# Two small matmul visits made into one, and two opening batches put in another order, in a fused attention and expert kernel

## The chip, the cores and the metric

One core of one Trainium2 chip. The metric is the device time of one execution in microseconds (us), median over several executions, the kernel before run on the same chip in the same rounds. The granted clock is the share of TensorE's full clock that the profile shows as granted, as a mean over an execution or a stretch. Times inside an execution are those of the profile, counted from the start of the span.

## The reference

```python
# q, k, v: (8 batches, 8 heads, 576 positions, 64)
scores = (q @ k.T) / 8
mask_local   = (rel >= 0) & (rel < 32)             # heads 0 to 3
mask_strided = (rel >= 0) & (pos_k % 32 == pos_q % 32)   # heads 4 to 7
attn = softmax(where(mask, scores, -1e9)) @ v
x = attn as (4608 tokens, 512)
h = x @ w_in                                       # 512 -> 2048
g = maximum(h, 0) + alpha * minimum(h, 0)
out = g @ w_out                                    # 2048 -> 512, float32
```

The sum of a softmax comes as a 65th column of v that is all ones, so after PV one reciprocal and one multiply on VectorE (DVE) divide.

## The kernel before

The expert part runs in nine chunks of 512 tokens: first layer in 16 groups (`hps`), second in 16 pieces (`ops`). Between them "pieces" of attention for later batches are slipped in: transposes (T), scores (S, two per head pair), PV (P, two or three per pair), transposes of the result (X). The kernel keeps the instructions of each engine in the order written. Pairs are numbered through the batches, four to a batch, so pairs 8 to 11 are batch 2. From batch 2 on, the results of three pairs of a batch are transposed by a transfer (`x_dma`) and that of the fourth by PE (X): of batch 2, `xs` holds pair 10, and X is done for pair 11. PSUM is split in three pools: `ps` (3 banks: PV, transposes), `hps` (3 banks) and `sp` (2 banks).

```python
def score_piece(P, i):                # a pair is two heads; i is the half of the positions
    sp = pbpool.tile([128, 2, 512], F32, tag="sp")
    ...
    for x, t in enumerate(grp):
        for y in range(2):            # two heads on the two 64-row halves of the array
            nc.tensor.matmul(sps[y][...], P.kT[64*y:64*y+64, ...], P.qT[64*y:64*y+64, ...])
    nc.scalar.activation(ev, sp, AF.Exp, scale=SCALE)         # ACT
    nc.gpsimd.tensor_tensor(ev, ev, m, op=ALU.mult)           # POOL: the mask

def pv_piece(P, a):
    pv = pspool.tile(...); ...        # matmuls
    nc.vector.reciprocal(rc, pv[..., 64])
    nc.vector.tensor_tensor(P.x16[...], pv[..., 0:64], rc, op=ALU.mult)

def lin1_piece(n, m):
    hps = phpool.tile(...); ...       # 4 matmuls
    nc.scalar.activation(neg, hps, AF.Relu, scale=-1.0)
    def fin(): nc.vector.scalar_tensor_tensor(gTs[n][:, m, :], neg, oma, hps, ...)  # frees hps
    late.append(fin)

def attn_step(end):
    if pos["i"] < end:
        pieces[pos["i"]][1]()         # one attention piece
        pos["i"] += 1
    while late:
        late.pop(0)()                 # then fin of the first-layer group

def x_dma(P):   ... nc.sync.dma_start_transpose(P.xs, P.x16[0:80, :])     # a strided pair
def x_copy(P):  ... nc.scalar.copy(xT[...], P.xs[...])                     # on ACT, later
```

The softmax here doesn't subtract the row's maximum and nothing guards it: scores larger than these inputs give would overflow.

## Time and profile before

| | us |
|---|---|
| time, median of 3 before the change was tried | 329.38 |
| span of the profiled execution, whose time was 328.5 | 326.6 |
| TensorE (PE) busy | 316.8 |
| first expert matmul starts | 26.56 |
| first layer of chunks 3 and 4 starts | 135.76 and 169.12 |

The distance between two chunks is the length of a steady cycle, 33.36 us, in which one batch of attention is slipped in.

### The profile page before, as it was taken

To read this page: it belongs to the slowest core of one execution; us is meant where nothing else is said; L and a number is where in the kernel's file an instruction comes from. 1 tells how busy PE (TensorE), PEld (TensorE's weight loads), DVE (VectorE), ACT (ScalarE), POOL (GpSimd) and SP (SyncE) were. 2 spreads that over 40 slices of the span, in tenths; PEclk is the share of its full clock that TensorE was granted. 3 is DMA by queue.
4 is the path that set the end of the run, shared out by engine and by line. 5 is a ranking of instruction groups with operands and counts; after the bars stand their busy time and mean duration, and the time that the engine had idled before them with its cause. 6 is when DMAs were issued, how large, how long until landed. Compare 5 with 4: busy or idle time off the path is not lost.

```text
span 326.6 us, 6269 instructions
## 1 busy us (share of the span) xinstructions
PE 316.8 (97%) x2493; PEld 161.8 (50%) x2493; DVE 182.8 (56%) x358; ACT 172.5 (53%) x295; POOL 141.2 (43%) x152
## 2 busy tenths in 40 slices
PE   7899999999998999999999999999999999999995
PEld 2454455554553445444568744445444444444444
DVE  5477835577543872488338832883377338505801
ACT  2744663368446754575467545764566347415610
POOL 8832495307996366736573638342513300000000
PEclk9999999999999999999999999999999999999999
DMA  6999999797499899686967496635530320021011
GB/s 222 198 206 207 243 210 170 115 258 167 90 155 155 214 81 153 118 212 74 160 109 222 59 143 116 109 43 101 122 76 0 55 91 25 1 91 40 0 64 64
DMA packets 77596, 40.32 MB, mean 123 GB/s; under 512 B 58480, under 2 KB 69248, under 8 KB 77568
## 3 DMA queue, kind: packets, MB, share of 16 engines
q0 software_dynamic: 41728, 17.38, 51.7%
q1 hardware_dynamic: 35840, 22.55, 28.5%
q8 instruction: 19, 0.31, 0.4%
q14 instruction: 9, 0.07, 0.1%
HBM read 38.01 MB, written 9.44 MB: 145 GB/s over the span
## 4 chain that ended last, share of the span: by engine, by line
PE 92%; DVE 3%; ACT 2%; DMA 2%; issue 0%; SPq 0%; DVEq 0%; ACTq 0%
PE hps L544 39%; PE ops L585 37%; PE sp L295 4%; PE pv L345 4%; PE tp L235 2%; DMA ql<-in_q_dram 2%; PE wps L607 1%; PE ops L577 1%; PE xp L362 1%; DVE x L354 1%; PE sph L311 1%; PE sp L311 1%; ACT kT L175 1%; DVE qT L177 1%; PE sph L295 1%; ACT qT L175 0%
## 5 line engine op out<-in xcount | busy, mean ns | idle before, releaser
L585 PE MATMUL ops<-wout,gT 128*128 128x512 f16 x560 | 137.7, 379 | 0.0
L557 DVE SCALAR_TENSOR_TENSOR gT<-neg,oma,hps 128x512 f16<-128x512 f32 x144 | 106.0, 745 | 54.6 <-ACT neg L554 47.1
L544 PE MATMUL hps<-xT,win 128*128 128x512 f16 (+1 forms) x640 | 133.4, 358 | 1.4 <-ACT xT L366 1.2
L554 ACT ACTIVATE neg<-hps 128x512 f32<-128x512 f32 x144 | 86.0, 597 | 41.0 <-PE hps L544 39.5
L329 POOL TENSOR_TENSOR et<-et,consts 128x576 f16<-128x576 f16 (+1 forms) x48 | 61.1, 1274 | 91.8 <-ACT et L319 91.8
L544 PEld LDWEIGHTS <-win 128*128 128x128 f16 x640 | 59.6, 98 | 57.6 <-issue 2.7
L585 PEld LDWEIGHTS <-gT 128*128 128x128 f16 x560 | 48.4, 97 | 45.6
L319 ACT ACTIVATE et<-sp 72x576 f16<-72x576 f32 (+1 forms) x56 | 36.2, 646 | 45.0 <-PE sp L295 36.7
L352 DVE RECIPROCAL rc<-pv 72x6 f32<-72x6 f32 (+2 forms) x80 | 14.8, 185 | 51.2 <-PE pv L345 51.2
L590 ACT COPY osb<-ops 128x512 f32<-128x512 f32 x35 | 20.5, 585 | 31.6 <-PE ops L585 31.2
L354 DVE TENSOR_TENSOR x<-pv,rc 96x384 f16<-96x384 f32 (+2 forms) x62 | 33.0, 532 | 2.1
L345 PEld LDWEIGHTS <-et 72*128 72x128 f16 (+1 forms) x448 | 23.2, 98 | 16.2 <-DVE x L354 1.1
L295 PEld LDWEIGHTS <-kT 64*128 64x128 f16 x448 | 10.8, 95 | 25.8 <-issue 20.7
L295 PE MATMUL sp<-qT,kT 64*128 64x72 f16 (+1 forms) x392 | 17.0, 201 | 1.9 <-ACT kT L175 1.9
L607 PE MATMUL wps<-wrm 128*128 128x512 f16 x44 | 16.1, 440 | 1.2 <-DVE wrm L619 1.2
L167 POOL DMA_DIRECT2D vl<-in_v_dram x8 | 11.2, 1397 | 9.9 <-PE pv L345 8.6
L345 PE MATMUL pv<-vs,et 72*128 72x65 f16 x256 | 15.3, 194 | 0.1
L177 DVE COPY qT<-tp 128x1024 f16<-128x1024 f16 (+1 forms) x10 | 10.1, 1011 | 7.9 <-PE tp L235 7.9
L179 POOL COPY vs<-stv 72x1024 f16<-72x1024 f16 x14 | 14.4, 1034 | 0.0
L383 ACT COPY xT<-xs 128x576 f16<-128x576 f16 x6 | 7.8, 1300 | 7.7 <-DMA xs<-x16s 7.7
L345 PE MATMUL pv<-vl,et 128*128 128x65 f16 x192 | 10.8, 194 | 0.0
L175 ACT COPY kT<-tp 128x1024 f16<-128x1024 f16 (+1 forms) x10 | 8.4, 843 | 3.9 <-PE tp L235 3.9
(72 smaller groups left out, 162.6 us busy)
## 6 DMA issues: line engine op xcount, KB each, us to landing
out_dram<-osb SPq DMA_DIRECT2D x35, 256.0 KB, 2.2
ql<-in_q_dram SPq DMA_DIRECT2D x6, 512.0 KB, 4.9
kl<-in_k_dram SPq DMA_DIRECT2D x6, 512.0 KB, 5.1
stv<-in_v_dram POOLq DMA_DIRECT2D x8, 288.0 KB, 6.4
vl<-in_v_dram POOLq DMA_DIRECT2D x6, 384.0 KB, 10.4
win<-in_moe_w_in_dram POOLq DMA_DIRECT2D x4, 512.0 KB, 9.3
wout<-in_moe_w_out_dram POOLq DMA_DIRECT2D x4, 512.0 KB, 16.6
qsd<-in_q_dram POOLq DMA_DIRECT2D x6, 288.0 KB, 5.7
```

What stands on the lines that cost most here:

```text
L295: keep(nc.tensor.matmul(sps[y][:, w * x : w * x + w], P.kT[hf, k0 : k0 + 128], P.qT[hf, q0 : q0 + w], start=(x == 0), stop=(x == len(grp) ...
L319: keep(nc.scalar.activation(ev.rearrange("r (y c) -> r y c", y=2), sp[0:r, :, 0:n], AF.Exp, scale=SCALE))
L329: keep(nc.gpsimd.tensor_tensor(ev, ev, m, op=ALU.mult))
L345: keep(nc.tensor.matmul(pv[:, 65 * x : 65 * x + 65], et[0:r, c : c + 128], v16[0:r, 2 * P.pr + hh, t, :] if P.strided else v16[:, 6 * (2 * ...
L352: keep(nc.vector.reciprocal(rc[0:w, 0:nb], pvv[:, :, 64]))
L354: keep(nc.vector.tensor_tensor(P.x16[0:w, c0 : c0 + 64 * nb].rearrange("r (c e) -> r c e", e=64), pvv[:, :, 0:64], rc[0:w, 0:nb].unsqueeze ...
L544: keep(nc.tensor.matmul(hps[:, dst : dst + w], win16[:, kk, 128 * m : 128 * m + 128], xT[:, kk, src : src + w], start=(kk == 0 and x == 0) ...
L554: keep(nc.scalar.activation(neg, hps, AF.Relu, scale=-1.0))
L557: keep(nc.vector.scalar_tensor_tensor(gTs[n][:, m, :], neg, oma[:, m : m + 1], hps, op0=ALU.mult, op1=ALU.add))
L585: keep(nc.tensor.matmul(ops, gTs[n][:, kf, 128 * mt : 128 * mt + 128], wout16[:, kf, :], start=(kf == 0), stop=(kf == 15)))
L590: keep(nc.scalar.copy(osb, ops))
L607: keep(nc.tensor.matmul(wps, wrm[:, 0:128], wrm, start=True, stop=True))
```

## The change

Its intent: each score piece puts TensorE into row-tiled mode and back, so do both pieces of a pair in one visit (batches 2 to 7), with the second half in banks of `ps` and its exponentials deferred, one by one, to the ends of this step and the next. In batches 0 and 1, start PV of the strided pairs between the transposes of the local ones, and let ACT do one of the local copies.

```diff
+    def score_both(P):
+        for i in range(2):
+            if i:
+                sps = [pspool.tile([128, 512], F32, tag="ps", name="sph") for _ in range(2)]
+            else:
+                sp = pbpool.tile([128, 2, 512], F32, tag="sp", name="sp")
...
+            if i == 0:
+                keep(nc.scalar.activation(..., sp[0:r, :, 0:n], AF.Exp, scale=SCALE))
+                keep(nc.gpsimd.tensor_tensor(mv, mv, m, op=ALU.mult))
+                continue
+            defer.extend([lambda: ex(0), lambda: ex(1)])     # halves on ACT, mask after the second
...
-            seq.append(("S", Sc(a, 0)))
+            seq.append(("S", lambda a=a: score_both(pairs[a])))
...
-        if okA:
-            seq.append(("S2", Sc(a, 1)))
...
-        copyP = next((i for i, z in enumerate(seq) if z[0] == "S2"), 0)
+        copyP = min(2, len(seq) - 1)
...
         while late:
             late.pop(0)()
+        if defer:
+            defer.pop(0)()
...
+        fns += [Pv(A[0], 0), T(u1, "q"), Pv(A[0], 1), T(u1, "k"), Pv(A[0], 2), Sc(L[0], 0), Sc(L[0], 1)]
+        fns += [lambda: (over_v(...), pv_piece(pairs[A[1]], 0)), Sc(L[1], 0), Pv(A[1], 1)]
...
```

More of the change, by code (lines that the diff above doesn't have):

```diff
@@ L329, in score_piece, with ex @@
         keep(nc.gpsimd.tensor_tensor(ev, ev, m, op=ALU.mult))
+    defer, defer_et = [], {}
+    def score_both(P):
+        w, r = P.w, 72 if P.strided else 128
+        for i in range(2):
+            et = ets[ectr["i"] % NE]
+            ectr["i"] += 1
+            if i:
+                sps = [pspool.tile([128, 512], F32, tag="ps", name="sph") for _ in range(2)]
+            else:
+                sp = pbpool.tile([128, 2, 512], F32, tag="sp", name="sp")
+                sps = [sp[:, y] for y in range(2)]
+            grp = P.sgroups[i]
+            n = w * len(grp)
+            for x, t in enumerate(grp):
+                if P.dx:
+                    q0 = k0 = 80 * (4 * (2 * P.pr + t % 2) + t // 2)
+                else:
+                    q0, k0 = w * t, 32 + 72 * t if P.strided else 96 * t
+                for y in range(2):
+                    hf = slice(64 * y, 64 * y + 64)
+                    keep(nc.tensor.matmul(
+                        sps[y][:, w * x : w * x + w], P.kT[hf, k0 : k0 + 128],
+                        P.qT[hf, q0 : q0 + w], start=(x == 0), stop=(x == len(grp) - 1),
+                        skip_group_check=True))
+                    P.et[(2 * (t // 2) + y, t % 2) if P.strided else (t, y)] = (et, n * y + w * x)
+            ev = et[0:r, 0 : 2 * n]
+            if not P.strided and i == 0:
+                mv = ev.rearrange("r (y c) -> r y c", y=2)
+                m = mfirst.unsqueeze(1).to_broadcast([r, 2, n])
+            else:
+                mv = ev.rearrange("r (c f) -> r c f", f=w)
+                m = (mstr if P.strided else mother).unsqueeze(1).to_broadcast([r, 2 * n // w, w])
+            if i == 0:
+                keep(nc.scalar.activation(
+                    ev.rearrange("r (y c) -> r y c", y=2), sp[0:r, :, 0:n], AF.Exp, scale=SCALE))
+                keep(nc.gpsimd.tensor_tensor(mv, mv, m, op=ALU.mult))
+                continue
+            def ex(y):
+                keep(nc.scalar.activation(
+                    ev[:, n * y : n * y + n], sps[y][0:r, 0:n], AF.Exp, scale=SCALE))
+                if y:
+                    keep(nc.gpsimd.tensor_tensor(mv, mv, m, op=ALU.mult))
+            defer_et["et"] = et
+            defer.extend([lambda: ex(0), lambda: ex(1)])
@@ L331, in pv_piece @@
     def pv_piece(P, a):
+        while defer and any(P.et[z][0] is defer_et["et"] for z in P.et):
+            defer.pop(0)()
         if P.x16 is None:
@@ L369, in x_piece @@
         else:
-            keep(nc.vector.tensor_copy(xT[:, P.hp, base : base + S], xp[:, 0:576]))
+            cast_copy("act" if P.b < NEARLY and P.hp == 0 else "dve",
+                      xT[:, P.hp, base : base + S], xp[:, 0:576])
     def x_dma(P):
@@ L404, in X, with alone @@
         return lambda: x_piece(pairs[g])
-    def alone(u0, u1, ahead):
+    def alone(u0, u1):
         A, L = (2 * u0, 2 * u0 + 1), (2 * u1, 2 * u1 + 1)
-        feed(T(u0, "q"), -1)
-        feed(T(u0, "k"), -1)
-        for g in A:
-            for i in range(2):
-                feed(Sc(g, i), -1)
-        if ahead:
-            feed(T(u1, "q"), -1)
-            feed(T(u1, "k"), -1)
-            for i in range(2):
-                feed(Sc(L[0], i), -1)
-        for g in A:
-            for i in range(3):
-                feed(Pv(g, i), -1)
-        if not ahead:
-            feed(T(u1, "q"), -1)
-            feed(X(A[0]), -1)
-            feed(T(u1, "k"), -1)
-            feed(X(A[1]), -1)
-            for i in range(2):
-                feed(Sc(L[0], i), -1)
-        for i in range(2):
-            feed(Sc(L[1], i), -1)
-        if ahead:
-            for g in A:
-                feed(X(g), -1)
-        for g in L:
-            for i in range(2):
-                if g == L[0] and i == 0:
-                    feed(lambda: (over_v(u0 // 2, "dve"), pv_piece(pairs[L[0]], 0)), -1)
-                else:
-                    feed(Pv(g, i), -1)
-        for g in L:
-            feed(X(g), -1)
-    alone(1, 0, True)
+        fns = [T(u0, "q"), T(u0, "k")] + [Sc(g, i) for g in A for i in range(2)]
+        fns += [Pv(A[0], 0), T(u1, "q"), Pv(A[0], 1), T(u1, "k"), Pv(A[0], 2), Sc(L[0], 0), Sc(L[0], 1)]
+        fns += [lambda: (over_v(u0 // 2, "dve"), pv_piece(pairs[A[1]], 0)), Sc(L[1], 0), Pv(A[1], 1)]
+        fns += [Sc(L[1], 1), Pv(A[1], 2), Pv(L[0], 0), X(A[0]), Pv(L[0], 1), X(A[1])]
+        fns += [Pv(L[1], 0), Pv(L[1], 1), X(L[0]), X(L[1])]
+        for fn in fns:
+            feed(fn, -1)
+    alone(1, 0)
     end0 = len(pieces)
-    alone(3, 2, True)
+    alone(3, 2)
     end1 = len(pieces)
@@ L529, in attn_step @@
             late.pop(0)()
+        if defer:
+            defer.pop(0)()
     gTs = {}
```

## The prediction

> **What bounds the kernel now.** I read the page first (busy time, the row of forty slices, the chain that ended last), then the sums by stretches of 20 us, then the chain in order of time, and last the timeline wherever the chain leaves TensorE.
>
> ```profile
> PE 316.8 (97%) x2493; PEld 161.8 (50%) x2493; DVE 182.8 (56%) x358; ACT 172.5 (53%) x295; POOL 141.2 (43%) x152
> ...
> PE 92%; DVE 3%; ACT 2%; DMA 2%; issue 0%; SPq 0%; DVEq 0%; ACTq 0%
> ```
>
> TensorE (PE) is 92% of the chain that ended last; no other engine is near full on average. So a change pays only if it shortens PE's own work, or removes one of the few waits of PE. Where are those? From the stretches (first value span, then PE busy):
>
> ```profile
> 0.00:20.00 20.00, 16.83 (x156) 8.38 (x157) 10.85 (x34) 9.03 (x18) 15.55 (x29) 1.00 1.22 209
> 20.00:40.00 20.00, 19.34 (x145) 9.52 (x145) 15.81 (x31) 10.81 (x20) 6.07 (x9) 1.00 1.25 214
> 40.00:60.00 20.00, 19.16 (x209) 10.62 (x208) 9.49 (x23) 10.40 (x24) 13.83 (x17) 1.00 1.76 194
> 60.00:80.00 20.00, 19.81 (x155) 10.10 (x154) 14.00 (x25) 12.39 (x23) 7.20 (x8) 1.00 1.05 196
> 80.00:100.00 20.00, 20.00 (x202) 10.42 (x201) 11.52 (x28) 8.13 (x14) 19.21 (x19) 1.00 1.15 118
> 100.00:120.00 20.00, 18.81 (x139) 8.68 (x137) 13.62 (x25) 15.03 (x25) 11.56 (x11) 1.00 0.70 149
> 120.00:140.00 20.00, 20.00 (x167) 9.86 (x165) 8.29 (x18) 10.50 (x17) 11.25 (x12) 1.00 1.40 133
> ```
>
> From 120 to 240 us PE has no idle time. Idle are 3.17 us at the start, 0.66 and 0.84 us in batches 0 and 1, 0.19 us in 60:80, 1.19 us just after 100 us. In 80:100 GpSimd (POOL, fifth engine) is 96% full, which matters below. Within the gapless part, the chain shows what a visit to attention costs the stream of expert matmuls:
>
> ```profile
> 111.39 1.73 PE hps L544 x8
> 113.12 0.24 PE sp L295 x8
> 113.36 1.83 PE hps L544 x8
> 115.19 0.18 PE pv L345 x6
> 115.38 1.73 PE hps L544 x8
> ```
>
> Eight expert matmuls of 512 columns take 1.73 us after a PV visit (L345), but 1.83 after a score visit (L295): a score visit costs about 0.10 us in the group beside it besides its own 0.24. A PV visit adds nothing beyond its 0.18 us.
>
> **What the Trainium skill says.** "TensorEngine Tiling (Array Packing)", section Key Properties: changing the tiling mode drains TensorE. Scores use 64-row halves (contraction over head_dim 64), all else uses the full array; the trace agrees, as single starts read from it show. The last expert matmul before a score visit starts at 154.506 us and the first score at 154.818: 0.312 us where the stream otherwise goes at 0.216, so 0.096 us lost going in. The last score pair starts at 154.923 and the next expert matmul at 155.054, 0.131 us later where the pairs are 0.033 apart, then 0.227 instead of 0.216 to the next: about 0.11 us coming out. "TensorE: Matmul & The Clock Gate", section The mechanism (Part 3), says matmuls of different row groups start about 4 ns apart; here the two halves of a head pair start 3 to 4 ns apart. Same page, section "Architectural detail: the array is 16× 32×32, not 1× 128×128", says ACT and DVE are strict FIFO; the trace shows a copy held behind another at 100 us (below). "PSUM — Partial Sum Buffer", section Specifications, gives 8 banks per partition; the kernel's pools hold all (3+3+2), which is why the second half of a merged visit must borrow banks of the pool that PV and transposes use.
>
> **The change, part by part.**
>
> Part 1, one visit per pair. From batch 2 on there are 6 x 4 = 24 head pairs, each with two score visits before and one after. A strided visit costs 0.24 + 0.10 = 0.34 us; of this its four concurrent pairs stream 4 x 0.034 = 0.135, so 0.205 us is entry and exit. A local visit: 0.23 + 0.10 = 0.33, three pairs about 0.045 apart, 0.135, so 0.195. Merged, the second half pays streaming only. All of it lies on PE, which is the path: 24 x 0.20 = **4.9 us** off.
>
> What it adds: the second half's exponential becomes two of 288 columns instead of one of 576. From batches 0 and 1: 0.41 us each with 0.29 between starts, so 0.70 for the two against 0.65 for one; 24 x 0.05 to 0.15 is under 4 us on ACT, which has 45% idle. It doesn't delay the evictions of the first layer: taking PE free after a first-layer group as zero, ACT's relu of that group occupies 0.2 to 0.7, the wide exponential 0.7 to 1.25, the first half 1.25 to 1.55, and the next group (0.475 us visit plus 0.863) is ready at 1.54. The other half is deferred behind the next relu, 2.03 to 2.33, and the next group is ready at 2.40. So no loss, provided the deferral works as written. Banks: the visit takes two of three in the shared pool. I followed the rotation through one batch; each taker comes at least one 0.86 us step after the half that frees its bank, so no regular wait.
>
> Part 2, batches 0 and 1. The end of batch 0 was a chain of DVE work, one multiply after another 0.69 us apart with a reciprocal between:
>
> ```profile
> 24.90 0.55 DVE x L354
> ...
> 25.59 0.57 DVE x L354
> ...
> 26.54 0.47 DVE xT L370
> ...
> 27.05 13.76 PE hps L544 x63
> ```
>
> Before, DVE starts its ten PV pieces at 17.93. The new order lets the first at 13.9, between the local transposes. I laid the new order out by hand with these durations (PV 0.20, warm-up matmul 0.22, score visit with mask about 0.69, transposed copies 0.69 DVE and 0.58 ACT): the local transposes' copies now queue behind PV's DVE work, local scores start about 16.7 instead of 16.04, four score visits and six PVs then alternate until about 21, and the last multiply ends near 24.75 instead of 26.16. The first expert matmul comes at about 25.65: **1.4 us** off. One local copy moved to ACT leaves DVE's tail. In batch 1 PE waits 0.37 and 0.47 us for the transposed copies; with PV pieces between, I expect **0.6 us** of the 0.84 back. The loads batch 1 needs landed by 39.2 us (issue 23 plus 15.8 and so on), used no sooner than 40.6, so they don't eat the gain.
>
> Part 3, pacing. A batch has 17 pieces in place of 21. At the start of batch 2 scores come two first-layer groups after the key transpose instead of one, which takes back the 0.2 to 0.3 us PE wait in 60:80: **0.25 us**.
>
> Part 4, given back in batch 2. The 1.19 us just after 100 us:
>
> ```profile
> 100.14 1.30 ACT L383 COPY xT<-xs 128x576 f16<-128x576 f16 x1 [3.73 <-DMA xs<-x16s]
> ...
> 101.35 0.58 ACT L590 COPY osb<-ops 128x512 f32<-128x512 f32 x1
> ...
> 101.83 0.65 ACT L319 ACTIVATE et<-sp 128x576 f16<-128x576 f32 x1
> ...
> 102.37 0.64 ACT L366 COPY xT<-xp 128x576 f16<-128x576 f16 x1
> ```
>
> ACT was held by a transposing transfer (6.3 us to landing), and everything queued behind it reached PE. After the change that transfer is issued about one second-layer step (1.15 us) earlier relative to the batch's end, but two more exponentials (0.6 us) stand before the last copy, and PE's own transpose now needs the bank that the first of them frees. By hand the stall becomes 1.75 us: **0.5 us** lost. And in 75:90, where POOL is nearly full, the second mask of a pair now queues behind casts (1.03 us each); PV of the first two pairs of batch 2 may wait 0.3 to 0.5 us for it twice, of which I count **0.5 us**.
>
> Sum: 4.9 + 1.4 + 0.6 + 0.25 - 0.5 - 0.5 = 6.15 us. 329.4 - 6.15 = **323.2 us**, 1.9% faster.
>
> **Rivals.**
> (a) Banks or ACT become the new wait: if a PV or transpose waits for the deferred half in each pair, 24 x 0.2 eats part 1, and the time is about 327 to 328. For it: two of three shared banks, and ACT's chain at 100 us. Against: ACT is 53% busy, and steps are 0.86 us apart.
> (b) Batch 0's gain is hidden because the start is bound by loads (DMA share 1.2 there): then about 324.6. For: the software queue is busy until 40 us. Against: the chain at 17 to 27 us is DVE and PE, with no transfer in it.
> (c) The batch 2 stall shrinks rather than grows, as the transfer lands sooner, and POOL keeps up: then 321.5 to 322.
>
> **Range and chances.** Part 1 is arithmetic on PE's path, good to 0.5 us. Parts 2 and 3 together 1.2 to 3.0; part 4 between +0.8 and -2.5. This gives 321.0 to 326.0 for eight in ten. 2% faster is 322.8, just beside my middle, with the losses more likely under- than overestimated: faster 0.42, within 2% 0.57, slower 0.01.
>
> **What would show it.** L295's successor should show 16 or 12 matmuls in one visit of about 0.37 us in the chain plus 0.10 beside it, 24 of them; a steady batch cycle should fall from 33.4 us (102.8 to 135.9 on to 169.3) by 0.8 us to about 32.6. The first expert matmul should start near 25.6 instead of 27.05, and the waits of PE for key copies in 40:60 mostly vanish. PE idle near the end of batch 2 should be 1.2 to 2.3 us, released by ACT. I am wrong if the steady cycle falls by less than 0.5 us (rival a), if the first expert matmul still starts at 27 (rival b), or if the batch 2 stall is gone (rival c).

## The result, and the profile after

| | before | changed |
|---|---|---|
| median of 6 executions each | 329.22 us | 328.01 us |
| ratio of means, 95% interval | | 0.9966 (0.9952 to 0.9979) |
| granted clock | 1.0 (profiled execution) | 0.993 to 0.995 (all six) |

A ratio here and below is the mean time of one kernel's runs over that of the other's runs of the same rounds, so not quite the ratio of the medians quoted. The change brings 0.3%, not 1.9%: 328.01 us lies above the range of 321.0 to 326.0, and the prediction is wrong.

Busy time and the chain by engine, changed kernel:

```profile
PE 314.9 (96%) x2493; PEld 162.9 (50%) x2493; DVE 182.4 (56%) x356; ACT 173.1 (53%) x321; POOL 140.8 (43%) x152
...
PE 85%; issue 4%; DMA 4%; DVE 2%; POOL 2%; ACT 1%; SPq 0%; POOLq 0%; ACTq 0%; DVEq 0%
```

The chain by engine has lost 7 points of PE and gained DMA and "issue" (time with no wait that the profile can name). The loss has a place. The same stretches as before, at the end of batch 2 (after the span the busy times of PE, PEld, DVE, ACT and POOL, then the granted clock, DMA share and GB/s):

```profile
80.00:100.00 20.00, 17.81 (x190) 9.45 (x191) 9.45 (x24) 6.95 (x15) 18.81 (x19) 1.00 0.98 118
100.00:120.00 20.00, 17.93 (x124) 8.14 (x124) 11.97 (x20) 13.72 (x27) 10.14 (x10) 0.91 0.81 160
```

Before, PE was idle there 0 and 1.19 us; now 2.19 and 2.07, and the clock of the second stretch is 0.91. The timeline of that place shows why (start, length, engine, line, operation; in brackets the idle time before and who ended it):

```profile
88.35 1.47 POOL L167 DMA_DIRECT2D vl<-in_v_dram  x1
...
90.89 1.63 SPq L428 DMA_TRANSPOSE xs<-x16s  x1
...
99.30 1.30 ACT L435 COPY xT<-xs 128x576 f16<-128x576 f16 x1 [6.54 <-DMA xs<-x16s]
...
100.98 0.66 ACT L366 ACTIVATE et<-sp 128x576 f16<-128x576 f32 x1
...
101.52 0.71 ACT L372 ACTIVATE et<-sph 128x288 f16<-128x288 f32 x2
...
101.99 0.42 PE L413 MATMUL xp<-consts,x 72*128 72x72 f16 x8 [4.02 <-ACT et L372]
```

Read it from below. PE's transposes of the pair's result (`xp`) wait 4.02 us for the first of two half exponentials, which frees their bank. That one stands in ACT's order behind a copy, and the copy waits 6.54 us for the transposing transfer `xs`: 8.4 us to landing. After this idle time the clock drops:

```profile
102.00:107.00 5.00, 5.00 (x23) 2.09 (x23) 0.75 (x1) 2.33 (x5) 4.19 (x4) 0.66 1.00 192
```

Single starts in the trace: from 102.99 to 105.98 us the expert matmuls are 0.427 us apart instead of 0.216. Seven such distances and a half-slowed one at each end cost 1.7 us in all. The Trainium skill, "TensorE: Matmul & The Clock Gate", section "HAM oscillation — how this bites in real kernels", puts the idle time after which the clock halves at about 3.4 us. These runs agree: 4.02 us of idle time here, and 4.16 us in the run with the merged visit alone below, are followed by 3 us of matmuls 0.427 us apart, and 1.32 us (late load) by none. An idle time between these was not seen in a profile here.

The second reading is the steady stream of the first layer, chain in order of time, changed kernel:

```profile
140.45 0.18 PE pv L396 x6
140.63 1.73 PE hps L570 x8
142.36 0.04 issue
142.40 1.02 PE hps L570 x4
143.42 0.24 PE sp L353 x8
143.66 0.13 PE sph L353 x8
```

A merged visit is there, 0.24 + 0.13 us, and the 0.10 beside it as before: 0.47. But the third group after a PV visit now starts 0.2 us late (0.04 of "issue", and 1.02 in place of 0.86), twice in each cycle. What DVE does just then, timeline of DVE:

```profile
140.92 0.18 DVE L403 RECIPROCAL rc<-pv 96x6 f32<-96x6 f32 x1
141.14 0.55 DVE L405 TENSOR_TENSOR x<-pv,rc 96x384 f16<-96x384 f32 x1
141.61 1.39 DVE L583 SCALAR_TENSOR_TENSOR gT<-neg,oma,hps 128x512 f16<-128x512 f32 x2
```

The first step of the last line ends near 142.36, and PE goes on at 142.40: the group needs the bank that this step frees, and PV's reciprocal and multiply stand ahead of it. In the kernel before, a score visit came two groups after PV and gave DVE 0.34 us.

Where the time went, from the starts of the stages (first matmul of each, single starts in the trace; chunk 0 is the first):

| starts at, us | before | changed | difference | change of it |
|---|---|---|---|---|
| first layer, chunk 0 | 26.56 | 25.23 | -1.33 | -1.33 |
| first layer, chunk 1 | 65.11 | 63.62 | -1.49 | -0.16 |
| second layer, chunk 1 | 81.81 | 80.30 | -1.51 | -0.02 |
| first layer, chunk 3 | 135.76 | 137.70 | +1.94 | **+3.45** |
| first layer, chunk 4 | 169.12 | 170.60 | +1.48 | -0.46 |
| first layer, chunk 6 | 235.99 | 236.54 | +0.55 | -0.93 |
| first layer, chunk 7 | 267.53 | 267.31 | -0.22 | -0.77 |

### The profile page after: what moved, and what is told of

Its sections match the earlier page's. It is cut to its first block, busy times and chain, and to the rows that moved or that the text cites. A ratio compares the mean times of both kernels' runs of the same rounds, so it can differ in the third digit from the quotient of the medians.

```text
span 326.4 us, 6321 instructions
## 1 busy us (share of the span) xinstructions
PE 314.9 (96%) x2493; PEld 162.9 (50%) x2493; DVE 182.4 (56%) x356; ACT 173.1 (53%) x321; POOL 140.8 (43%) x152
## 4 chain that ended last, share of the span: by engine, by line
PE 85%; issue 4%; DMA 4%; DVE 2%; POOL 2%; ACT 1%; SPq 0%; POOLq 0%; ACTq 0%; DVEq 0%
PE hps L570 35%; PE ops L611 34%; PE pv L396 4%; DMA xs<-x16s 3%; PE tp L235 2%; PE wps L633 2%; DMA ql<-in_q_dram 2%; PE sp L353 1%; PE ops L603 1%; PE xp L413 1%; PE sp L311 1%; PE sph L311 1%; PE sph L353 1%; DVE x L405 1%; DVE qT L177 1%
## 5 line engine op out<-in xcount | busy, mean ns | idle before, releaser
L611 PE MATMUL ops<-wout,gT 128*128 128x512 f16 x560 | 135.7, 380 | 0.0
L570 PEld LDWEIGHTS <-win 128*128 128x128 f16 x640 | 60.6, 98 | 60.7 <-issue 5.3
L611 PEld LDWEIGHTS <-gT 128*128 128x128 f16 x560 | 49.2, 98 | 47.2
L396 PEld LDWEIGHTS <-et 72*128 72x128 f16 (+1 forms) x448 | 24.1, 98 | 16.6 <-POOL et L375 0.9
L366 ACT ACTIVATE et<-sp 128x576 f16<-128x576 f32 (+1 forms) x24 | 15.5, 646 | 10.6 <-PE sp L353 10.6
L372 ACT ACTIVATE et<-sph 128x288 f16<-128x288 f32 (+1 forms) x48 | 18.6, 409 | 0.0
L353 PEld LDWEIGHTS <-kT 64*128 64x128 f16 x336 | 7.1, 95 | 9.9 <-issue 8.9
L417 ACT COPY xT<-xp 128x576 f16<-128x576 f16 x10 | 6.4, 639 | 10.1 <-PE xp L413 10.1
```

Source lines behind the costliest of these rows:

```text
L366: keep(nc.scalar.activation(ev.rearrange("r (y c) -> r y c", y=2), sp[0:r, :, 0:n], AF.Exp, scale=SCALE))
L372: keep(nc.scalar.activation(ev[:, n * y : n * y + n], sps[y][0:r, 0:n], AF.Exp, scale=SCALE))
L396: keep(nc.tensor.matmul(pv[:, 65 * x : 65 * x + 65], et[0:r, c : c + 128], v16[0:r, 2 * P.pr + hh, t, :] if P.strided else v16[:, 6 * (2 * ...
L570: keep(nc.tensor.matmul(hps[:, dst : dst + w], win16[:, kk, 128 * m : 128 * m + 128], xT[:, kk, src : src + w], start=(kk == 0 and x == 0) ...
L611: keep(nc.tensor.matmul(ops, gTs[n][:, kf, 128 * mt : 128 * mt + 128], wout16[:, kf, :], start=(kf == 0), stop=(kf == 15)))
```

## The experiments

My theory: two side effects eat the gain. (A) At the end of batch 2, `xs` lands late because the loads of POOL's software queue fill the transfer engines beside it; ACT's order carries that to the exponentials, and the merged visit's borrowed banks carry it to PE. (B) In the first layer, PV's DVE work holds a bank too long once no score visit follows. Rivals: the merged visit saves little by itself; the wait is one for banks whatever ACT does; the new order of the batches is at fault. Each kernel was timed in five rounds; "before" of the same rounds has a median of 329.1 to 329.25 us. Times of different sets are from different chips. Some of before's executions, 4 of 11 in the first set and 1 of 11 in each of the two others, took about 331 us with a clock of 0.995; they count too, so ratios lean a little low.

### One part alone

Order only: the kernel before with the new `alone` and the one copy on ACT.

```diff
-    alone(1, 0, True) ... alone(3, 2, True)     # old order
+    alone(1, 0) ... alone(3, 2)                 # new order; scores still one by one
```

> The kernel before with only the new order of batches 0 and 1 (and the one local copy moved to ACT). Theory (the xs transfer of batch 2 lands at a time set by the loads beside it, not by when it is issued): first expert matmul near 25.7 us, but PE's wait near 100 us grows from 1.2 to 2 to 2.7 us, so 328.0 to 329.2 us. Rival (the order gain is kept whole): 327.6 to 327.9 us, wait near 100 us still 1.2.

Measured: 327.08 us, ratio 0.9915 (0.9884 to 0.9947). First expert matmul at 25.14 us, the next at 25.64, which is the one that the expectation counts (see part 2 below). `xs` landed 7.1 us after its issue, at 99.4 where before it was 100.1, although issued 1.6 us earlier. The wait near 100 us grew from 1.19 to 0.73 + 1.19 = 1.92 us, just under what I expected; the total missed the expectation by 1 us on the good side, and the rival's too. The profiled execution is 0.8 us of span under before's, while the medians differ by 2.1. The profiled execution was the slowest of its six (327.76 us), and before's (328.5 us) lies 0.7 us under its median. So both traces make the gain look smaller than it is, and the wait in a usual execution of this kernel may be shorter.

Merged visit only: the changed kernel with the old order, and the one local copy back on DVE.

```diff
-    alone(1, 0) ... alone(3, 2)
+    alone(1, 0, True) ... alone(3, 2, True)
```

> The changed kernel with the old order of batches 0 and 1: one score visit per pair alone. Theory (bank and ACT block at X of pair 11, DVE wait after PV in the first layer): each batch cycle from 3 to 6 falls by 0.45 us, not 0.8; PE waits 2 to 3.5 us before X of pair 11; total 327.5 to 329 us. Rival (merging itself saves its 4.9 us and the loss in the changed kernel comes from the new order): 324 to 325 us.

Measured: 329.89 us, ratio 0.999 (0.9951 to 1.0028), nothing gained. PE waits 4.16 us before X of pair 11, more than I expected, `xs` lands in 8.5 us, and the clock is 0.987 to 0.995 in five executions of six. The sixth, at full clock, took 327.52. The cycle from chunk 3 to 4 is 32.90. The total is 0.9 us above my range. So the loss is there without the new order; the merged visit brings it.

### The wait at the end of batch 2

One load moved out of the way of the transfer:

```diff
-    if g % 4 == 2 and c + 2 < B:
+    if g % 4 == 2 and c + 2 < B and c != 2:
         load_v(c + 2, False)
+    if g == 13:
+        load_v(4, False)
```

> The changed kernel with one load moved: local v of batch 4 is issued in iteration 13 instead of 10, out of the way of the transposing transfer xs of batch 2. Theory (xs lands late because the software queue is full beside it): xs lands in 3 to 5 us instead of 8.4, PE's wait of 4.0 us before X of pair 11 falls under 0.7 us, the clock stays full, total 323 to 324.5 us. Rival (the transfer is slow for another reason, or the wait is one for banks whatever ACT does): wait stays above 3 us, 327.5 to 328.5 us.

Measured: 323.79 us, ratio 0.9814 (0.9784 to 0.9844), clock 0.998 to 1.0. Timeline at that place:

```profile
90.84 1.32 SPq L428 DMA_TRANSPOSE xs<-x16s  x1
...
96.54 1.30 ACT L435 COPY xT<-xs 128x576 f16<-128x576 f16 x1 [3.84 <-DMA xs<-x16s]
...
99.23 0.42 PE L413 MATMUL xp<-consts,x 72*128 72x72 f16 x8 [1.32 <-ACT et L372]
```

`xs` lands in 5.7 us, not 8.4, and PE waits 1.32 us. The total is what the theory said, the wait is longer than it said (under 0.7); the loads of q and k of the next batch are still beside the transfer, which may be why. Moving one load, with nothing of the change undone, brings 4.2 us by the medians (of different rounds, whose medians of before are both 329.22); by the traces 2.7 us less waiting and 1.7 us of clock.

Now ACT's order alone, transfer and loads untouched:

```diff
-    if copyp and ...:
+    if copyp and g != 12 and ...:
         x_copy(pairs[g - 2])
+    if g == 13 and kind == "X":
+        x_copy(pairs[10])           # behind the copy of X of pair 11
```

> The changed kernel with ACT's copy of xs of batch 2 put behind the copy of X of pair 11 in ACT's order, transfer and loads untouched. Theory (strict order on ACT: the exponentials that free PE's bank stand behind a copy that waits for the transfer): no wait of PE before X of pair 11; instead the first layer waits for the third quarter of its input until about 100.6 us, 1 to 2.5 us; total 325.5 to 327 us. Rival (the bank wait comes from two of three banks being taken, not from ACT's order): a wait over 3 us before X remains, 327.5 to 328.5.

Timeline of this kernel at that place:

```profile
97.76 0.42 PE L413 MATMUL xp<-consts,x 72*128 72x72 f16 x8
...
99.50 1.31 ACT L435 COPY xT<-xs 128x576 f16<-128x576 f16 x1 [0.64 <-DMA xs<-x16s]
...
100.86 2.32 PE L572 MATMUL hps<-xT,win 128*128 128x512 f16 x10 [1.38 <-ACT xT L435]
```

The transfer is as slow as before (8.6 us), two of three banks are taken as before, and yet `xp` waits for nothing: what remains is the true need, 1.38 us until the first layer's input is there. 323.71 us, ratio 0.9816 (0.9781 to 0.9851), 1.8 us under the expected range. The clock stayed at 0.998 to 1.0, and its 1.7 us I had not counted. The rival of the banks falls. Another wait, 0.66 us for the keys of batch 3, appears later.

The same load moved in the kernel before:

```diff
-    if g % 4 == 2 and c + 2 < B:
+    if g % 4 == 2 and c + 2 < B and c != 2:
         load_v(c + 2, False)
+    if g == 13:
+        load_v(4, False)
```

> The kernel before with the same one load moved as in the changed kernel with the late load. Theory (the transfer next to that load also cost the kernel before its 1.2 us near 100 us, and its executions at 331 us with a lower clock are those in which the wait grew past what keeps the clock): wait near 100 us under 0.5 us, 328 to 328.5 us, and no executions near 331. Rival (the load matters only to the changed kernel): 329.2 as before, with executions near 331.

Timeline of SP's queue and of ACT:

```profile
93.64 1.21 SPq L376 DMA_TRANSPOSE xs<-x16s  x1
```

```profile
96.68 1.31 ACT L383 COPY xT<-xs 128x576 f16<-128x576 f16 x1 [0.50 <-DMA xs<-x16s]
```

Landing in 3.0 us instead of 6.3, no wait of PE near 100 us, no execution over 327.2: 326.99 us, ratio 0.9926 (0.9902 to 0.995), 1 us better than expected. So the kernel before had the same illness in a mild form. Whether its executions near 331 us came of it is not shown: in these rounds only 1 of before's 11 was one, so none in six says little. And compare the landings: with that load away, `xs` lands at 96.7 us here, issued at 93.64, and at 96.5 us in the changed kernel, issued at 90.84. Issuing it 2.8 us earlier brought 0.2 us. In both, the loads of q and k of the next batch landed at 92.3 to 94.9 us, shortly ahead of it. So the landing hardly follows the issue. That the moved load delayed it is shown in both kernels; that the loads of q and k set what is left is argued from these times alone. Nor do the runs tell whether loads slow `xs` itself or the output store ahead of it in SP's queue, which landed 7.4 us after its issue in the changed kernel and 4.6 us with the load moved.

### The waits in the first layer

DVE's step for the first layer goes ahead of PV's work, on top of the late load:

```diff
     def attn_step(end):
+        while late:
+            late.pop(0)()
         if pos["i"] < end:
             pieces[pos["i"]][1]()
             pos["i"] += 1
-        while late:
-            late.pop(0)()
         if defer:
             defer.pop(0)()
```

> The changed kernel with the late load, and with the last step of a first-layer group on DVE put ahead of the reciprocal and multiply of a PV piece of the same step. Theory (in each batch cycle two waits of 0.2 us of PE for a first-layer bank come from PV's DVE work standing ahead of that step; 33.35 before became 32.90 instead of 32.5): cycle near 32.5 us, total about 321.8 to 322.5 us. Rival (the 0.4 us per cycle is something else, such as ACT or the merged visit itself): cycle stays 32.9, total 323.5 to 324 us.

Chain in order of time:

```profile
140.82 0.18 PE pv L396 x6
141.01 2.59 PE hps L572 x12
143.59 0.18 PE pv L396 x6
```

Twelve matmuls after PV take 2.59 us (12 times 0.216) with nothing lost; the cycle from chunk 3 to 4 is 133.10 to 165.61, 32.51 us, as expected. 322.12 us, ratio 0.9775 (0.9746 to 0.9805).

The suspected cost made smaller instead of moved: PV without the division, a wrong result.

```diff
-        keep(nc.vector.reciprocal(rc[0:w, 0:nb], pvv[:, :, 64]))
-        keep(nc.vector.tensor_tensor(P.x16[...], pvv[:, :, 0:64], rc..., op=ALU.mult))
+        keep(nc.vector.tensor_copy(P.x16[...], pvv[:, :, 0:64]))
```

> The changed kernel with the late load and without the division: PV is copied by one DVE instruction, without reciprocal (a wrong result on purpose). Takes about 0.2 us of DVE from each PV piece and leaves its order. Theory (DVE's work for PV holds the first-layer bank 0.2 us too long): the waits after PV shrink from 0.2 to under 0.05 us, cycle 32.5 to 32.6 us. Rival: the waits of 0.2 us stay. Batch 0 ends earlier too, so the total says less: 320.5 to 322.5 us.

Measured: cycle 131.51 to 164.02, 32.50 us by the unrounded starts, the waits after PV gone, 320.41 us. With the order untouched, less DVE work for PV does the same as putting it later: it is DVE's time that PE waited for.

The control, late load and DVE order in the kernel before:

```diff
+    (the late load, as above)
     def attn_step(end):
+        while late:
+            late.pop(0)()
         if pos["i"] < end:
             pieces[pos["i"]][1]()
             pos["i"] += 1
-        while late:
-            late.pop(0)()
```

> The kernel before with the late load and with the DVE step of the first layer ahead of PV's: a control. Theory (the kernel before had a score visit after each PV in the first layer, which gave DVE the time it needed, so there is nothing to win by the DVE order): cycle stays 33.3 to 33.4 us, 326.8 to 327.3 us, as with the late load alone. Rival (the DVE order is worth 2 us in any kernel): 324.5 to 325.3 us.

Measured: 326.70 us, ratio 0.9924 (0.9906 to 0.9943), cycle 134.45 to 167.81, 33.35, as before. Against the late load alone the median is 0.3 us lower, which is not resolved, as the two come from different rounds and chips; the traces show a gain of 0.4 us in chunk 6, which has only two pairs left and so few score visits already (from its first to its second layer 15.21 us in place of 15.60).

### What the merged visit is worth, and the best version

Merged visit, old order, with late load, late copy and DVE order:

```diff
-    alone(1, 0) ... alone(3, 2)
+    alone(1, 0, True) ... alone(3, 2, True)
+    (the late load, the late copy and the new attn_step, as above)
```

> One score visit per pair with the old order of batches 0 and 1, with late load, late copy and DVE step first. Against the control this is the merged visit with its two side effects removed. Theory (24 visits at 0.2 us, less 0.4 to 0.6 us waiting for masks and for the transfer in batch 2): 322.4 to 323.3 us, 4.0 to 4.6 us under the control, and 1.2 to 1.6 us over the version with the new order. Rival (merging brings under 3 us even then): above 324 us.

Measured: 323.10 us, ratio 0.9813 (0.9792 to 0.9835), 3.6 us under the control, where I expected 4.0 to 4.6. (The control has no late copy, but no wait near 100 us either.) Left over are a wait of 0.52 us for a mask in batch 2 and one of 0.63 for `xs`.

All of it with the new order:

```diff
     alone(1, 0) ... alone(3, 2)
+    (the late load, the late copy and the new attn_step, as above)
```

> Late load, late copy and the DVE step first together, a correct kernel meant to beat both. If the late load leaves the transfer landing near 96.5 us, the copy no longer blocks ACT and the first layer waits for nothing: 320.8 to 321.8 us. If moving the copy costs as much as it saves once the load is late: 321.8 to 322.5 us.

Measured: 321.54 us (321.29 to 321.56), ratio 0.9758 (0.9729 to 0.9787), correct. It beats both kernels, and is 1.6 us under the version with the old order (1.2 to 1.6 expected; other rounds): that is what the new order is worth once the waits are gone; the waits of PE after 38 us are 0.64, 0.52, 0.37 and 0.14 us. Its first layer of chunk 3 starts at 132.38, 5.3 us ahead of the changed kernel's.

## Why the prediction was wrong

Point by point, in its order.

**Part 1, size of a visit: right.** A merged visit costs 0.24 + 0.13 + 0.10 = 0.47 us against the 0.475 that I worked out. (24 x 0.20 is 4.8 us, not the 4.9 of the sum.) **"So no loss, provided the deferral works as written": wrong.** The deferral worked, but that step looked at ACT and at the banks of the shared pool only. DVE also has to free the bank of each first-layer group, and it was left out. A cycle fell by 0.46 us, not 0.8, and so by less than the 0.5 that the prediction itself named as the sign of being wrong. Two waits of 0.2 us on DVE are the rest, and the two experiments on DVE bring the cycle to 32.51 and 32.50, 0.85 under before. Over chunks 2 to 5 that is about 1.6 us. The score visits that were removed had been covering DVE's work.

**Part 2, batch 0: right** (1.33 for 1.4), and by the path foreseen: DVE's last multiply ends at 24.81 us, where 24.75 was worked out and 26.14 stood before. The 27.05 us that the prediction calls the first expert matmul is the second one; the first starts at 26.56. The second now starts at 25.73, for 25.65. **Batch 1: mis-sized** (0.16 for 0.6). The wait of 0.37 us ahead of the strided scores stayed, since the order changes only after them; the trace shows it at 43.29 where before it was at 44.62. The one of 0.47 shrank to 0.14 us ahead of the tail transposes, whose bank a copy on ACT still held. So 0.33 us of waiting went, but the stage shrank by 0.16 only; where the other half went is not shown.

**Part 3, pacing: right in kind.** The 0.17 us at 74 us is gone. **In part 4, the mask wait is right** (0.39 us at 79.7 for 0.5), and it eats part 3.

**Part 4, the end of batch 2: the step that failed most.** I expected PE to wait at X for the bank that the first half exponential frees, and it does. But I took the 6.3 us to landing with me, as if it were the transfer's own, with the transfer issued "about one second-layer step (1.15 us) earlier relative to the batch's end". It was issued 3.0 us earlier (90.89, before 93.87) and landed only 0.8 us earlier (99.3, before 100.1). Counted from the start of chunk 1's second layer, where the changed kernel is 1.5 us ahead, it was issued 1.5 us earlier and landed 0.7 us later. The 6.3 us was not a property of the transfer (3.0 with one load moved) but of the loads beside it, which POOL issues nearly when it did before (v at 88.35, before 89.07). So the wait became 4.02 us, not 1.75, and with it the clock dropped, another 1.7 us that stood nowhere in my sum. From the second layer of chunk 1 to chunk 3 the kernel lost 3.45 us where the merged visits of batch 3 and of the rest of batch 2 should have won; with both fixes and the late copy that stretch is 132.38 - 80.44 = 51.94 us, 5.46 less than in the changed kernel.

The trace itself ends 0.2 us under before, while the medians differ by 1.2 us: most of that is the choice of executions, as before's profiled one (328.5 us) was 0.7 us faster than before's median. Of the rivals, (a) was half right: a new wait did eat part of each cycle, but through DVE, not ACT or the shared pool; these two made the wait at the end of batch 2. (b) falls, batch 0 kept its gain. (c) was the wrong way round. Not tried: whether loading q and k of batch 3 later would bring `xs` to 3 us in the changed kernel too.

## What to carry to other kernels

Work taken off the busiest engine is also time taken from the engines that freed buffers meanwhile: before counting it as gained, check for each of them what it frees next, not just the one that the change touches. A transfer's time to landing belongs to its neighbours in the queues as much as to itself; take it from the trace together with what loads beside it, and keep an instruction that waits for it out of the way of those that free a busy engine's buffers. And a long wait can cost more than itself: after the 4.02 us here the clock took another 1.7 us, after the 1.32 us of the late load nothing.

## What the Trainium skill lacked or had wrong

- "TensorEngine Tiling (Array Packing)", Key Properties, says that switching drains TensorE, without a figure. Here a visit to 64-row mode costs 0.2 us of entry and exit (0.34 us with 8 small matmuls, 0.47 with 16).
- "DMA: Bandwidth & Descriptors", section Issuing engines are not separate DMA queues, says that transfers of all engines interleave, and agrees with these runs (a load of POOL's queue moved away brought a transfer of SP's queue from 8.4 to 5.7 us); it has no figure for a transposing transfer beside loads. Here the same transfer of an 80 x 1024 tile lands in 2.7 us in the median, and in 3.0 to 8.6 us at the end of batch 2, by what was loading.

No passage that is cited here was found wrong.
